# An HGRN2 attention block and a SwiGLU block in one kernel: half copies of v, score copies, transposed output and the order of the crossed matmuls

## The chip, the cores and the metric

The kernel runs on one core of a Trainium2 chip. The metric is the device time of one execution in microseconds (us); less is better. The engines of the core work side by side, each through its own list of instructions in order: TensorE (PE; its weight loads are shown as PEld), VectorE (DVE), ScalarE (ACT), GpSimd (POOL) and SyncE (SP). SP and POOL issue most of the DMA transfers here. PE writes its results to PSUM, whose eight banks the program hands out through pools; ACT and DVE read them there.

## The reference

A gated linear recurrence over 768 steps for 4 batches and 8 heads of 48 channels, and a SwiGLU block behind it. All is float32.

```python
f = 1.0 / (1.0 + np.exp(-f_logit))              # q, k, v, f_logit: (4, 8, 768, 48)
for t in range(S):
    state = f[:, :, t, :, None] * state + np.einsum('bhd,bhe->bhde', k[:, :, t], v[:, :, t])
    y[:, :, t] = np.einsum('bhd,bhde->bhe', q[:, :, t], state)
x = y.transpose(0, 2, 1, 3).reshape(B * S, H * D)     # (3072, 384)
g = x @ w_gate                                        # (384, 1536)
out = (g * sigmoid(g) * (x @ w_val)) @ w_out          # (1536, 384)
```

## The kernel before

**Chunks and units.** The 768 steps are cut into six chunks of 128. A unit u is one batch b in one chunk c; u = 4c + b. For each unit the program turns the gates into running products, scales keys and queries with them, and multiplies: scores = keys x queries inside the chunk (masked to be causal), y = scores x v plus queries x the state of the chunk before, and a new state from keys and v. The MLP of chunk c - 1 (mlp_plain for chunk 0; mlp_fifteen and down_seven with fewer products for the others) runs on the same engines at the same time as the attention of later chunks.

**Order.** Attention is written as a generator (`attention(u)`, from line 624) that yields at 15 points. Tables of due times (EARLY for chunk 1, `times(c)` for chunks 2 to 5) say between which steps of the MLP each of these pieces is written, and `in_order` then fixes the order of each engine's list as written (in the part up to chunk 1 without POOL). So the order within PE, ACT, DVE and SP is that of the code; an instruction that waits holds up all behind it on its engine. The steps that matter here, in their order: qT (the scaled queries) and, in chunk 1, decayed (the state scaled by the gates); scores; masking; y; the rest of y; the new state.

**Units in halves.** In chunks 1 to 5 the first three batches (`in_halves`) treat each chunk as two halves of 64 steps, so that the quadrants of the PE array work side by side: K and M of 48 or 64. For these units the masked scores of a tile A (128 x 2 x 4 x 128) hold, for each parity `par` of the heads, 6 x 64 columns: four blocks on the diagonal, which a mask multiplies (DVE, line 795), and two blocks below it, which need no mask. From chunk 2 on the latter are plain copies on ACT (line 792); in chunk 1 DVE multiplies them by ones. Both stand in the step of masking, 0.9, 1.5 or 2 units of the planner's time behind that of the scores.

**v and its half copies.** Half of the A products need v with its halves of time exchanged, in the other 64 partitions. These copies are loaded beside v (line 504) into tiles of their own that `make_lower` sets aside: for chunk 1 inside the weight-sum tile `extra`, which is free until then, later in a tile `lower`. Their columns 48 to 64 are set to zero.

**y on PE** (lines 813 to 841): first, from chunk 2 on, the new state dS (8 matmuls, from kt, the transposed keys, which come back from DRAM by DMA); then the state part of y for the heads that lie in the right partitions ("own"), then 16 A products. In the step after, `rest_of_y`, come the state parts of the other heads ("crossed": 2 x 4 matmuls of 32 columns), the copies of y to yT (ACT, line 849), and ten DMA transfers for the columns of the chunk into xT, the input of the MLP (line 856). From chunk 2 on that step is due 0.03 behind y, and the next unit's scores 0.02, so that the scores stand between them. In chunk 1 dS comes in the step `rest_of_y`, ahead of the crossed matmuls.

**Room for yT.** In chunk 1 yT and `diagonal` (the state of the fourth batch, laid out for full-array matmuls) share one buffer of tag x. Later both take a buffer of the ring of three, tag aside, into which ACT copies products of the MLP.

**Banks.** From chunk 2 on the scores take banks of the MLP's own tags (o or A) in most units, so the next product with that tag waits until DVE and ACT have read the scores.

Names in the profile: L754 and L760 write scores (sc), L833 the state part of y, L841 the A products of units in halves, L867 the y of fourth batches, L813 dS, L1150 the products of the MLP and L1253 its down products. "x16" in a row counts the two passes that PE makes for each float32 matmul.

Of the kernel before, what the change touches and what calls it, by code (L numbers as in the profile page):

```python
# [290 lines left out]
def short_path(ctx, tc, ident, least, judge, q, k, v, f_logit, moe_w_gate, moe_w_val, moe_w_out, out):  # L291
# [9 lines left out]
    nc = tc.nc  # L301
# [110 lines left out]
    CH = C // 2  # L412
    lower = [], []

    def make_lower(room, masks, late):
# [12 lines left out]
        lower[late][:] = vs_, masks  # L428

    def other_v(u):  # L430
        at = lower[units[u][1] >= SQUARES][0]
        return at[u % 2 if units[u][1] >= SQUARES else units[u][0]]

    room = extra.rearrange("p e n j t -> p e (n j t)")
    make_lower([room[:, 4, i * HP * W:(i + 1) * HP * W] for i in range(B - 1)], room[:, 2, 0:(HP + HP // 2) * CH], False)

# [39 lines left out]
    def load(u, what="fkqv"):  # L476
# [3 lines left out]
        for nm in "fqkv" if c >= SQUARES else "fvkq" if by_squares(u) else "fkqv":  # L480
# [19 lines left out]
            queue.dma_start(out=dst[:, :, 0:D], in_=src[b, :, rows, :].rearrange("h t d -> t h d"))  # L500
            if nm == "v" and in_halves(u):
                for n in range(2):
                    since = c * C + (1 - n) * CH
                    queue.dma_start(out=other_v(u)[n * CH:(n + 1) * CH, :, 0:D],
                                    in_=src[b, n * HP:(n + 1) * HP, since:since + CH, :].rearrange("h t d -> t h d"))

# [117 lines left out]
    def attention(u):  # L624
# [13 lines left out]
        in_squares = by_squares(u)  # L638

        def multiply(out, x, by):  # L640
# [105 lines left out]
        yield  # L746

        sc = [score_bank(u) for _ in range(2)]
        halves = in_halves(u)
        for keys in range(2) if halves else ():  # L750
# [5 lines left out]
        for a in () if halves else range(HP):  # L756
            for par in range(2):
                r = rows_of(par)
                for half in range(2) if c else ():
                    nc.tensor.matmul(sc[par][W * half:W * half + W, a * C:(a + 1) * C], lhsT=kT[r, a, W * half:W * half + W],  # L760
                                     rhs=qT[r, a, :], start=True, stop=True)
                if c == 0:
                    nc.tensor.matmul(sc[par][:, a * C:(a + 1) * C], lhsT=kT[r, a, :], rhs=qT[r, a, :], start=True, stop=True)
# [9 lines left out]
        yield  # L773
        if u != SQUARES * B:
            A = att.tile([128, 2, HP, C], FP32, tag="A", name="A")
        flat = A.rearrange("p r a t -> p r (a t)")
        if not in_squares:
# [6 lines left out]
        if halves:  # L784
            first, rest = slice(0, HP * CH), slice(HP * CH, (HP + HP // 2) * CH)
            masks = lower[c >= SQUARES][1]
            if c < SQUARES:
                first = slice(0, rest.stop)
            else:
                masks = masks.unsqueeze(1).broadcast_to((128, HP, CH))  # L790
                for par in range(2):
                    nc.scalar.copy(flat[:, par, rest], sc[par][:, rest])
            for par in range(2):
                by_head = [t if len(t.shape) == 3 else t[:, first].rearrange("p (a t) -> p a t", t=CH) for t in (flat[:, par], sc[par], masks)]
                nc.vector.tensor_tensor(*by_head, ALU.mult)
# [21 lines left out]
        if halves:  # L817
# [11 lines left out]
            def of_state(pars_of, parts, first):  # L829
                for part in parts:  # L830
                    for a in range(HP):
                        par = pars_of(a)
                        nc.tensor.matmul(place(a, par, part), lhsT=decayed[rows_of(par), a, part], rhs=qT[rows_of(par), a, :],  # L833
                                         start=first, stop=not first, skip_group_check=True)

            of_state(lambda a: a // 2, [slice(0, W)], True)
            for keys in range(2):
                for par in range(2):
                    for a in (0, 2, 1, 3):
                        h, top = 2 * a + par, a // 2  # L840
                        nc.tensor.matmul(queries_of_keys(place(a, par), keys), rhs=blocks_of_keys(flat[:, par], top, a, keys),  # L841
                                         lhsT=(v_[:, h, :] if keys == top else other_v(u)[:, h % HP, :])[top * CH:(top + 1) * CH],
                                         start=False, stop=keys == 1 and par == top, skip_group_check=True)
# [42 lines left out]
        if halves:  # L886
            rest_of_y()
        if c >= SQUARES and u + 2 < len(units):
# [130 lines left out]
    def times(c):  # L1019
# [3 lines left out]
        masks = {"b": 2, "o": 0.9, "A": 1.5}  # L1023
        return [[f, *steps, s + 0.02, s + masks[kind], s + 2.2, o, o + (0.03 if b < B - 1 else 0.01), o + 2.1]
                for b, (f, steps, (s, kind), o) in enumerate(zip(sigmoid, CHAINS[c], SCORES[c], outputs))]

# [391 lines left out]
    make_rooms(comb)  # L1418
    room = comb.tile([128, 2 * HP * W + CH], FP32, tag="lower", name="lower")
    make_lower([room[:, i * HP * W:(i + 1) * HP * W] for i in range(2)], room[:, 2 * HP * W:], True)  # L1420
    load(SQUARES * B)
# [107 lines left out]
```

## Time and profile before

| | |
|---|---|
| time, median of 3 runs (us) | 594.83 (594.12 to 596.44) |
| profiled execution: its time, its span (us) | 594.78, 593.1 |
| ACT copies of scores, line 792 | 24 x 283 ns |
| DVE masking, line 795, chunks 2 to 5 | 24 x 416 ns |
| ACT copies to yT, line 849 | 30 x 374 ns |
| DMA transfers out of yT from POOL: issue, issue to landing | 0.50 us, 3.2 us |

The page of the profile gives busy times as shares of the span and the costliest groups of instructions. A row of the timeline has start, length, engine, line, operation, what is written from what, the number of instructions, and in brackets the idle time of the engine just before with what ended it. A row of the view of waits has who waited for whom, the total in us, how often, and the longest. Matmuls are pipelined, so their lengths overlap: the time that one takes from the engine is the distance to the next start.

### The profile page before, as it was taken

Reading aid. Unit: us, or ns where it says so; the run is one execution under the profiler, and the core shown is the slowest. Engines: PE = TensorE matmul, PEld = TensorE weight load, DVE = VectorE, ACT = ScalarE, POOL = GpSimd, SP = SyncE. Lnnn points to the kernel's source line nnn. Section 1 sums busy time; section 2 is a strip of 40 time slices with the busy share of each in tenths; the row PEclk is TensorE's granted clock in tenths of the full one; section 3 lists DMA queues with packets and bytes.
Section 4 is the critical chain, followed back from the end, with each engine's and each line's share of the span. In section 5 each row is a group of like instructions: output and inputs, shape, how many; then the busy total and the mean of one; then the engine's idle time right before and its main releaser. Section 6 shows DMA issues by size and latency. Waiting matters only on the chain.

```text
span 593.1 us, 12331 instructions
## 1 busy us (share of the span) xinstructions
PE 577.1 (97%) x4644; PEld 476.7 (80%) x4644; DVE 471.6 (80%) x828; ACT 307.1 (52%) x589; POOL 119.2 (20%) x262
## 2 busy tenths in 40 slices
PE   7899999999989999999999999999999999999996
PEld 5744444557878999878899988899988899988996
DVE  7988998999989977988995978995878972666641
ACT  3587787023877522666741486742376830356600
POOL 6140344201132150030330030311030321000000
PEclk9999999999999999999999999999999999999999
DMA  9999696234659566443444443344341100100001
GB/s 217 257 289 259 197 247 155 62 92 128 130 119 146 106 151 165 111 108 73 113 102 104 135 106 71 89 106 106 104 114 28 28 8 8 54 1 2 0 1 56
DMA packets 117825, 64.48 MB, mean 109 GB/s; under 512 B 75568, under 2 KB 108144, under 8 KB 117760
## 3 DMA queue, kind: packets, MB, share of 16 engines
q1 hardware_dynamic: 105360, 48.29, 33.1%
q0 software_dynamic: 11248, 13.78, 10.3%
q10 hardware_dynamic: 1152, 1.57, 0.7%
q8 instruction: 37, 0.61, 0.4%
q14 instruction: 28, 0.23, 0.1%
HBM read 49.64 MB, written 8.65 MB: 98 GB/s over the span
## 4 chain that ended last, share of the span: by engine, by line
PE 77%; DVE 7%; DMA 5%; ACT 3%; issue 3%; POOL 2%; SPq 1%; DVEq 0%; ACTq 0%; POOLq 0%
PE o L1253 19%; PE A L1150 16%; PE B L1150 13%; PE o L1150 5%; PE c L1150 5%; PE o L1316 3%; DMA xT<-yT 2%; PE y L867 2%; PE o L957 2%; PE gate L934 2%; DMA kt<-turn 2%; PE val L934 2%; PE dS L813 1%; PE sc L754 1%; PE y L833 1%
## 5 line engine op out<-in xcount | busy, mean ns | idle before, releaser
L856 POOL DMA_DIRECT2D xT<-yT x120 | 59.5, 505 | 71.7 <-ACT yT L849 62.3
L1150 PE MATMUL A<-xs,w_both 128*128 128x256 f32 x240 | 61.9, 380 | 1.3 <-ACT aside L1155 1.3
L1253 PE MATMUL o<-w_out,h 128*128 128x192 f32 x360 | 62.0, 327 | 0.0
L1253 PEld LDWEIGHTS o<-w_out,h 128*128 128x128 f32 x360 | 58.8, 190 | 0.9 <-issue 0.4
L1155 ACT COPY aside<-A 128x512 f32<-128x512 f32 x60 | 35.1, 584 | 34.9 <-PE A L1150 32.5
L1051 DVE TENSOR_TENSOR c<-c,aside 128x512 f32<-128x512 f32 x60 | 41.2, 686 | 13.7 <-ACT aside L1155 12.1
L1150 PEld LDWEIGHTS A<-xs,w_both 128*128 128x128 f32 x240 | 45.2, 190 | 8.1 <-ACT aside L1155 1.7
L1155 ACT COPY c<-A 128x512 f32<-128x512 f32 x40 | 23.3, 583 | 45.2 <-PE A L1150 45.2
L1102 DVE TENSOR_TENSOR h<-h,c 128x256 f32<-128x256 f32 x100 | 40.5, 413 | 6.1 <-ACT h L1166 5.8
L1054 DVE TENSOR_TENSOR c<-c,aside 128x512 f32<-128x512 f32 x60 | 41.0, 683 | 2.3 <-ACT aside L1155 2.2
L1253 PE MATMUL o<-ws,h 128*128 128x192 f32 x240 | 41.7, 328 | 0.0
L1166 ACT ACTIVATE h<-c 128x256 f32<-128x256 f32 x100 | 39.2, 416 | 4.7 <-DVE c L1051 3.5
L1150 PE MATMUL A<-xs,extra 128*128 128x256 f32 x160 | 41.2, 380 | 0.2 <-ACT c L1155 0.2
L1150 PE MATMUL B<-xs,w_both 128*128 128x256 f32 x160 | 41.2, 380 | 0.0
L1150 PE MATMUL c<-xT,w_both 128*128 128x256 f32 x160 | 41.1, 379 | 0.0
L1150 PE MATMUL B<-xT,extra 128*128 128x256 f32 x160 | 41.1, 379 | 0.0
L1155 ACT COPY aside<-B 128x512 f32<-128x512 f32 x60 | 35.1, 585 | 10.0 <-PE B L1150 6.6
L1253 PEld LDWEIGHTS o<-ws,h 128*128 128x128 f32 x240 | 39.3, 190 | 1.0 <-issue 0.8
L743 POOL MEMSET gates<- 128x4 f32 x24 | 3.7, 152 | 164.7 <-DVE qT L646 159.6
L1051 DVE TENSOR_TENSOR c<-c,o 128x384 f32<-128x384 f32 x15 | 8.2, 549 | 34.2 <-PE o L1253 34.2
L1054 DVE TENSOR_TENSOR c<-o,c 128x512 f32<-128x512 f32 x40 | 27.3, 684 | 9.3 <-ACT h L1166 5.8
L1150 PEld LDWEIGHTS A<-xs,extra 128*128 128x128 f32 x160 | 30.3, 190 | 4.7 <-ACT c L1155 0.6
(181 smaller groups left out, 1261.8 us busy)
## 6 DMA issues: line engine op xcount, KB each, us to landing
fsquares<-in_f_logit_dram SPq DMA_DIRECT2D x64, 96.0 KB
qsquares<-in_q_dram SPq DMA_DIRECT2D x64, 96.0 KB
ksquares<-in_k_dram SPq DMA_DIRECT2D x64, 96.0 KB
w<-in_moe_w_gate_dram SPq DMA_DIRECT2D x6, 768.0 KB
w<-in_moe_w_val_dram SPq DMA_DIRECT2D x6, 768.0 KB
w<-in_moe_w_out_dram SPq DMA_DIRECT2D x6, 768.0 KB
v<-in_v_dram SPq DMA_DIRECT2D x19, 192.0 KB
kt<-turn SPq DMA_DIRECT2D x12, 256.0 KB
```

What stands on the lines that cost most here:

```text
L856: (nc.gpsimd if c >= SQUARES else nc.sync).dma_start(out=xT[c][f % 128:f % 128 + n, f // 128, b * C:(b + 1) * C], in_=yT[r:r + n, a // 2, ...
L867: nc.tensor.matmul(y[Q * (n % 4):Q * (n % 4) + Q, n // 4 * C:(n // 4 + 1) * C], lhsT=lhsT, rhs=rhs, start=n % 4 not in met, stop=last, ski ...
L934: nc.tensor.matmul(p, lhsT=w[:, j, i, :], rhs=xT[c][:, i, :], start=(i == 0), stop=(i == KT - 1))
L957: nc.tensor.matmul(p, lhsT=hidden_tile(h, n // 2)[:, n % 2 * 2 + b // 2, b % 2 * C:(b % 2 + 1) * C], rhs=w_out[:, j, :], start=(n == 0), s ...
L1051: nc.vector.tensor_tensor(dst, a, b, ALU.add)
L1054: nc.vector.tensor_tensor(dst, a, b, ALU.subtract)
L1102: lagging.append(lambda: f(*args))
L1150: nc.tensor.matmul(p[name][:, n, :], lhsT=weights_of[a][:, n, j, :], rhs=tokens[b], start=fresh and n == 0, stop=True, skip_group_check=True)
L1155: nc.scalar.copy(t, p[name])
L1166: nc.scalar.activation(dst, src[:, 0, :], AF.Silu)
L1253: nc.tensor.matmul(p[:, n, :], lhsT=lhsTs[j][:, n * C:(n + 1) * C], rhs=rhs[:, j, :], start=first and j == order[0] and n == 0, stop=j == ...
L1316: nc.tensor.matmul(p, lhsT=hidden_tile(h, j)[:, 2, n * C:(n + 1) * C], rhs=b22[:, j, :], start=j == order[0], stop=j == order[-1])
```

## The change

1. The half copies of v (`load_other_v`) go into columns of A that the masked scores leave free: the two parities now lie at 0 to 384 and 384 to 768 of 1024 columns, and the last 256 hold four heads of v. They are loaded when A is handed out: with qT in chunk 1, with the scores later. Only 48 of 64 columns are loaded and used as stationary operand, so nothing is set to zero. The tiles of `make_lower` are gone, the masks stay (`make_diagonals`).
2. The ACT copies of the blocks below the diagonal stand right behind the scores instead of in the step of masking.
3. yT has a tile of its own (tag x in `att`); `diagonal` of chunk 1 takes a buffer of the ring in which weights are loaded (w64, four buffers).
4. The crossed matmuls run first, then dS (in chunk 1 too), the own state part, and the A products. The step that follows only copies y and starts the transfers; it is due 0.01 behind y, ahead of the next unit's scores.

```diff
-        vs_ = [t.rearrange("p (h d) -> p h d", h=HP) for t in room]
-        for t in vs_:
-            nc.gpsimd.memset(t[:, :, D:W], 0.0)
+    def other_v(A):
+        return A.rearrange("p r a t -> p (r a t)")[:, 12 * CH:].rearrange("p (h e) -> p h e", e=W)
+    def load_other_v(A, u):
+        b, c = units[u]
+        queue = nc.sync if c >= SQUARES or not by_squares(u) else nc.gpsimd
+        for n in range(2):
+            since = c * C + (1 - n) * CH
+            queue.dma_start(out=other_v(A)[n * CH:(n + 1) * CH, :, 0:D],
+                            in_=v[b, n * HP:(n + 1) * HP, since:since + CH, :].rearrange("h t d -> t h d"))
...
         def aside_room(name):
             if c < SQUARES:
-                return first_pool.tile([128, 2, TB // 2], FP32, tag="x", name=name)
+                return wst.tile([128, 2, TB // 2], FP32, tag="w64", name=name, bufs=4)
...
+        if halves and c < SQUARES:
+            A = att.tile([128, 2, HP, C], FP32, tag="A", name="A")
+            load_other_v(A, u)
         multiply(qT, qp, pairs(gate)[:, :, 1:N1])
...
+        flat = [A.rearrange("p r a t -> p (r a t)")[:, 6 * CH * par:6 * CH * par + 8 * CH] for par in range(2)]
+        if halves and c >= SQUARES:
+            load_other_v(A, u)
         sc = [score_bank(u) for _ in range(2)]
...
+        for par in range(2) if halves and c >= SQUARES else ():
+            nc.scalar.copy(flat[par][:, rest], sc[par][:, rest])
...
-                for par in range(2):
-                    nc.scalar.copy(flat[:, par, rest], sc[par][:, rest])
...
-            if c >= SQUARES and c < NCH - 1:
-                dS = new_state()
...
-            of_state(lambda a: a // 2, [slice(0, W)], True)
+            of_state(lambda a: 1 - a // 2, [slice(0, Q), slice(Q, W)], True)
+            if c < NCH - 1:
+                dS = new_state()
+            of_state(lambda a: a // 2, [slice(0, W)], False)
...
-                                         lhsT=(v_[:, h, :] if keys == top else other_v(u)[:, h % HP, :])[top * CH:(top + 1) * CH],
+                                         lhsT=(v_[:, h, :] if keys == top else other_v(A)[:, h % HP, 0:D])[top * CH:(top + 1) * CH],
...
-            def rest_of_y():
-                of_state(lambda a: 1 - a // 2, [slice(0, Q), slice(Q, W)], False)
-                yT = aside_room("yT")
+            def copy_y():
+                yT = att.tile([128, 2, TB // 2], FP32, tag="x", name="yT")
...
-        return [[f, *steps, s + 0.02, s + masks[kind], s + 2.2, o, o + (0.03 if b < B - 1 else 0.01), o + 2.1]
+        return [[f, *steps, s + 0.02, s + masks[kind], s + 2.2, o, o + 0.01, o + 2.1]
```

What this does to the lists of the engines, at three places. (A line's number is about 6 higher in the changed file.)

PE, first unit of chunk 2, before: the start of the block of y between two products of the MLP (A and B are also names of banks; y<-A is an A product, the tile v_124 is v).

```order
L1150 MATMUL B<-xT,extra 128x256 x2
L1150 MATMUL A<-xT,w_both 128x256 x2
L813 MATMUL dS<-v_124,kt 64x48 x8
L833 MATMUL y<-qT,decayed 64x128 x4
L841 MATMUL y<-A,v_124 64x128
L841 MATMUL y<-A,lower 64x128
```

PE, the same block, before: its end, with the next unit's scores (sc) and the crossed matmuls (32x128).

```order
L841 MATMUL y<-A,lower 64x64
L841 MATMUL y<-A,v_124 64x64
L754 MATMUL sc<-qT,kT 64x2x64 x8
L754 MATMUL sc<-qT,kT 64x64 x8
L833 MATMUL y<-qT,decayed 32x128 x8
L1150 MATMUL A<-xs,w_both 128x256 x2
```

PE, the same place, changed: the start of the block.

```order
L1156 MATMUL A<-xT,w_both 128x256 x2
L837 MATMUL y<-qT,decayed 32x128 x8
L819 MATMUL dS<-v_124,kt 64x48 x8
L837 MATMUL y<-qT,decayed 64x128 x4
L848 MATMUL y<-A,v_124 64x128
L848 MATMUL y<-A 48x128
```

The crossed matmuls have moved from the end, behind the scores, to the start; the products with the half copies write 48 rows instead of 64.

ACT at the same place, before: copies of y, a product of the MLP (c), a scaling of weights (ws), and then the copies of the scores.

```order
L668 ACTIVATE fsquares<-fsquares 128x16x32
L849 COPY yT<-y 128x256 x2
L1155 COPY c_1706<-A 128x512
L1089 ACTIVATE ws_1369<-ws_1368 128x1152
L792 COPY A<-sc 128x128 x2
L1155 COPY c_1718<-B 128x512
```

ACT, the same place, changed.

```order
L671 ACTIVATE fsquares<-fsquares 128x16x32
L855 COPY yT<-y 128x256 x2
L775 COPY A<-sc 128x128 x2
L1161 COPY c_1702<-A 128x512
L1095 ACTIVATE ws_1360<-ws_1359 128x1152
L1161 COPY c_1711<-B 128x512
```

The copies of the scores have moved ahead of the product's copy and of the scaling.

SP, chunk 2, between the second and the third unit, before: loads of q, the transposed keys kt, then v.

```order
L492 DMA ksquares<-in_k_dram 32x4x192 x4
L492 DMA qsquares<-in_q_dram 32x4x192 x4
L772 DMA kt<-turn 128x1x512
L500 DMA v_125<-in_v_dram 128x8x48
L492 DMA fsquares<-in_f_logit_dram 32x4x192 x4
```

SP, the same place, changed.

```order
L498 DMA ksquares<-in_k_dram 32x4x192 x4
L498 DMA qsquares<-in_q_dram 32x4x192 x4
L506 DMA v_125<-in_v_dram 128x8x48
L454 DMA A<-in_v_dram 64x4x48 x2
L784 DMA kt<-turn 128x1x512
L498 DMA fsquares<-in_f_logit_dram 32x4x192 x4
```

The transfer of kt now stands behind the load of v and the two half copies.

More of the change, by code (lines that the diff above doesn't have):

```diff
@@ L412, in short_path, with make_diagonals @@
     CH = C // 2
-    lower = [], []
-    def make_lower(room, masks, late):
+    diagonals = {}
+    def make_diagonals(masks, late):
         for n in range(2):
@@ L424, in make_lower @@
             nc.gpsimd.memset(masks[:, HP * CH:], 1.0)
-        vs_ = [t.rearrange("p (h d) -> p h d", h=HP) for t in room]
-        for t in vs_:
-            nc.gpsimd.memset(t[:, :, D:W], 0.0)
[L428 to L432, printed above, removed]
+        diagonals[late] = masks
     room = extra.rearrange("p e n j t -> p e (n j t)")
-    make_lower([room[:, 4, i * HP * W:(i + 1) * HP * W] for i in range(B - 1)], room[:, 2, 0:(HP + HP // 2) * CH], False)
+    make_diagonals(room[:, 2, 0:(HP + HP // 2) * CH], False)
     def in_halves(u):
@@ L500, in load @@
             queue.dma_start(out=dst[:, :, 0:D], in_=src[b, :, rows, :].rearrange("h t d -> t h d"))
[L501 to L505, printed above, removed]
     def weight_piece(dst, src, parts, signs):
@@ L638, in attention @@
         in_squares = by_squares(u)
+        halves = in_halves(u)
+        first, rest = slice(0, HP * CH), slice(HP * CH, (HP + HP // 2) * CH)
         def multiply(out, x, by):
@@ L746, in attention @@
         yield
+        if u != SQUARES * B and not (halves and c < SQUARES):
+            A = att.tile([128, 2, HP, C], FP32, tag="A", name="A")
+        flat = [A.rearrange("p r a t -> p (r a t)")[:, 6 * CH * par:6 * CH * par + 8 * CH] for par in range(2)]
+        if halves and c >= SQUARES:
+            load_other_v(A, u)
         sc = [score_bank(u) for _ in range(2)]
-        halves = in_halves(u)
         for keys in range(2) if halves else ():
@@ L784, in attention @@
         if halves:
-            first, rest = slice(0, HP * CH), slice(HP * CH, (HP + HP // 2) * CH)
-            masks = lower[c >= SQUARES][1]
+            masks = diagonals[c >= SQUARES]
             if c < SQUARES:
@@ L790, in attention @@
                 masks = masks.unsqueeze(1).broadcast_to((128, HP, CH))
-                for par in range(2):
-                    nc.scalar.copy(flat[:, par, rest], sc[par][:, rest])
             for par in range(2):
-                by_head = [t if len(t.shape) == 3 else t[:, first].rearrange("p (a t) -> p a t", t=CH) for t in (flat[:, par], sc[par], masks)]
+                by_head = [t if len(t.shape) == 3 else t[:, first].rearrange("p (a t) -> p a t", t=CH) for t in (flat[par], sc[par], masks)]
                 nc.vector.tensor_tensor(*by_head, ALU.mult)
@@ L833, in of_state @@
                         nc.tensor.matmul(place(a, par, part), lhsT=decayed[rows_of(par), a, part], rhs=qT[rows_of(par), a, :],
[L834 to L836 removed]
+                                         start=first, stop=False, skip_group_check=True)
+            of_state(lambda a: 1 - a // 2, [slice(0, Q), slice(Q, W)], True)
+            if c < NCH - 1:
+                dS = new_state()
+            of_state(lambda a: a // 2, [slice(0, W)], False)
             for keys in range(2):
@@ L1418, in short_path @@
     make_rooms(comb)
-    room = comb.tile([128, 2 * HP * W + CH], FP32, tag="lower", name="lower")
-    make_lower([room[:, i * HP * W:(i + 1) * HP * W] for i in range(2)], room[:, 2 * HP * W:], True)
+    make_diagonals(comb.tile([128, CH], FP32, tag="diagonals", name="diagonals"), True)
     load(SQUARES * B)
```

11 lines of the change are left out of this document (4 added, 7 removed).

## The prediction

> **What bounds the kernel now.** I read the page first, for who is busy.
>
> ```profile
> span 593.1 us, 12331 instructions
> PE 577.1 (97%) x4644; PEld 476.7 (80%) x4644; DVE 471.6 (80%) x828; ACT 307.1 (52%) x589; POOL 119.2 (20%) x262
> ```
>
> TensorE (PE) is busy for 577.1 of 593.1 us. Only two things can change the time: the 16.0 us in which PE idles, and what PE itself has to do. So I asked next where the idle time lies, by stretches of 60 us (length, then busy us of PE, PEld, DVE, ACT, POOL, the granted clock, DMA share, GB/s).
>
> ```profile
> 0.00:60.00 60.00, 54.44 (x445) 33.27 (x446) 49.83 (x82) 38.10 (x63) 18.95 (x59) 1.00 0.98 257
> 120.00:180.00 60.00, 56.82 (x412) 43.53 (x411) 53.86 (x97) 34.23 (x65) 11.75 (x25) 1.00 0.51 121
> 240.00:300.00 60.00, 58.48 (x458) 51.00 (x456) 53.71 (x99) 39.64 (x84) 10.22 (x23) 1.00 0.41 94
> 300.00:360.00 60.00, 60.00 (x583) 54.87 (x583) 48.48 (x86) 27.96 (x57) 11.23 (x24) 1.00 0.46 112
> 540.00:593.00 53.00, 47.91 (x264) 45.16 (x262) 26.75 (x47) 15.93 (x35) 0.00 (x0) 1.00 0.05 16
> ```
>
> 5.6 us of the idle time are at the start, 5.1 after the last matmul, 3.2 between 120 and 180, 1.5 between 240 and 300. From 300 on PE has no gap, so nothing that a faster ScalarE, VectorE or DMA does there can show. The clock is 1.00 everywhere and plays no part. The view of waits, for PE alone, names the gaps (total us, times, longest):
>
> ```profile
> PE sc L763 <- DVE qT L646: 2.4, 2, 1.6
> PE o L1150 <- DVE A L795: 1.5, 1, 1.5
> PE y L867 <- ACT diagonal L658: 1.4, 1, 1.4
> PE A L1150 <- ACT aside L1155: 1.3, 1, 1.3
> PE dS L813 <- DMA kt<-turn: 0.3, 1, 0.3
> ```
>
> The first belongs to chunk 0, which the change leaves as it is. The other four are at places that the change touches, and the sum is made of them and of two of 0.26 us whose rows stand further down.
>
> **The diagonal tile (a tile of its own for yT).** Before, yT and diagonal of chunk 1 share one buffer.
>
> ```profile
> 116.18 0.35 DVE L652 TENSOR_TENSOR decayed<-state,least 128x192 f32<-128x192 f32 x1
> 122.77 0.51 ACT L656 COPY diagonal<-spare 128x384 f32<-128x384 f32 x1 [11.39 <-DMA xT<-yT]
> 123.72 1.12 PE L867 MATMUL y<-qT,diagonal 128*32 128x128 f32 x21 [1.35 <-ACT diagonal L658]
> 126.64 0.43 DVE L1054 TENSOR_TENSOR xs<-xT 128x256 f32<-128x256 f32 x1 [1.19 <-ACT xT L882]
> ```
>
> ScalarE has been idle for 11.39 us until the last transfer out of yT lands, and PE waits 1.35 us. Now diagonal takes a weight buffer and yT has its own. Its other input, decayed, is done at 116.53, so diagonal could be ready near 117.8 against the 122.4 at which PE wants it: the wait goes, with 4.6 us to spare. What could be late next is VectorE, which idles 1.19 us before xs for the same chain and then works off the sums for the next stage. The next time that it idles, it waits for PE:
>
> ```profile
> 142.22 0.69 DVE L1054 TENSOR_TENSOR c<-o,c 128x512 f32<-128x512 f32 x1 [1.07 <-PE o L1150]
> ```
>
> So it starts 1.19 us sooner and has 1.07 us in hand: I count the full 1.35.
>
> **The copies right behind the scores.** At the second unit of chunk 2, PE needs a bank of tag o that still holds scores.
>
> ```profile
> 170.32 0.68 DVE L1051 TENSOR_TENSOR c<-c,aside 128x512 f32<-128x512 f32 x1
> 172.11 1.17 ACT L1089 ACTIVATE ws<-ws 128x1152 f32<-128x1152 f32 x1
> 173.17 0.42 ACT L792 COPY A<-sc 128x128 f32<-128x128 f32 x2
> 173.46 0.76 DVE L795 TENSOR_TENSOR A<-sc,lower 128x256 f32<-128x256 f32 x2 [2.45 <-ACT A L792]
> 173.94 1.13 PE L1150 MATMUL o<-xT,w_both 128*128 128x256 f32 x4 [1.49 <-DVE A L795]
> ```
>
> In ScalarE's order the copies stand behind a product's copy and the 1.17 us ws; VectorE's masking waits 2.45 us for them, and PE 1.49. Now they stand ahead of both. Scores end near 170.1, the copies (0.42 us) near 170.6, and VectorE is free at 171.0, so its 0.76 us end near 171.75 while PE wants the bank near 171.9. I count 1.49. The copies delay what is behind them by 0.42 us each time; the sum of ScalarE's work is unchanged, and it is busy 34.23 of 60 us here. By the same ordering the third product's B bank is freed about 0.1 us late; I charge 0.1.
>
> **yT out of the ring of aside tiles.**
>
> ```profile
> 263.32 0.58 ACT L1155 COPY aside<-A 128x512 f32<-128x512 f32 x1 [2.26 <-DMA xT<-yT]
> 263.96 1.13 PE L1150 MATMUL A<-xs,w_both 128*128 128x256 f32 x4 [1.25 <-ACT aside L1155]
> ```
>
> One of three aside buffers was held by yT until its transfers landed. With yT elsewhere ScalarE could have copied 2.26 us earlier: 1.25 us gained. The single new yT buffer must be free again when the next unit's copy comes; I return to that among the rivals.
>
> **The crossed matmuls first.** The chain of work shows one unit's block on PE (start, length):
>
> ```profile
> 278.90 0.60 PE dS L813 x16
> 279.50 0.38 PE y L833 x8
> 279.88 0.67 PE y L841 x32
> 280.55 0.67 PE sc L754 x32
> 281.22 0.38 PE y L833 x16
> ```
>
> The last 0.38 us, the crossed matmuls, moves to the front; the same rows run, 2.70 us in all. What changes is when each piece starts: dS, own state and A products stay or come later, and the next unit's scores start 0.38 us later, yet nothing runs behind them. Where scores waited for a bank or for qT, the crossed matmuls now fill that wait.
>
> ```profile
> 168.75 1.40 PE L754 MATMUL sc<-qT,kT 48*64 48x128 f32 x32
> 203.88 0.85 PE L754 MATMUL sc<-qT,kT 48*64 48x128 f32 x32
> 213.07 1.10 PE L760 MATMUL sc<-qT,kT 48*64 48x128 f32 x32 [0.26 <-DVE qT L646]
> 250.88 0.89 PE L754 MATMUL sc<-qT,kT 48*64 48x128 f32 x30 [0.26 <-DVE c L1054]
> ```
>
> The first row takes 1.40 us against an undisturbed 0.85, a hidden wait of 0.5; the last two show 0.26 each beside a stretched start. At each of the three the gain is at least 0.26 and at most the 0.38 us moved: I take 0.38, since the release by VectorE does not move; 1.14 in all.
>
> The same order costs something in chunk 1, where dS ran last but one and is now second.
>
> ```profile
> 104.53 0.71 POOL L781 DMA_DIRECT2D kt<-turn  x1 [0.86 <-issue]
> 108.11 0.45 PE L833 MATMUL y<-qT,decayed 48*64 48x128 f32 x8
> 109.56 0.67 PE L813 MATMUL dS<-v,kt 128*64 128x48 f32 x16 [0.34 <-DMA kt<-turn]
> DMA to landing us min/median/max: 4.9/5.2/12.3
> ```
>
> At the third unit kt lands about 109.5. Before, own state and A products (1.05 us) ran ahead of dS and PE waited 0.34. Now only 0.38 us stand ahead, so PE waits about 1.0 us: a loss of 0.66. It is zero only if kt's transfer starts earlier; POOL has two more transfers to issue for this unit, but long before, so I expect no shift either way.
>
> **Half copies of v.** The bytes stay (two transfers of 48 KB a unit). At the start POOL no longer issues four and SP two; PE's 5.6 us there hang on the VectorE and ScalarE chain of chunk 0, so nothing is gained. From chunk 2 on, both transfers wait on SP until PE has left A, behind the load of v, and kt's transfer now stands behind all three: about 2 us later. Nearly everywhere 13 us or more lie between. The tight place is the third unit of chunk 2:
>
> ```profile
> 203.06 0.57 SPq L772 DMA_DIRECT2D kt<-turn  x1
> 211.09 0.67 PE L813 MATMUL dS<-v,kt 128*64 128x48 f32 x16
> ```
>
> SP can start v at 204.3, when the A products end, so by its rows (0.4 for v, 0.65 for each half) kt is issued near 206.1 to 206.7. No view gives SP's landing time; bounds from POOL's transfers of the same shape are 4.9 and 12.3, and I take the median of 5.2: it lands near 211.9 at the worst, against dS at 211.5. I charge 0 and keep up to 7 us as the bad end.
>
> The crossed A products use stationary operands of 48 columns where it was 64. The profile has no such row; the nearest are the rows of 48 partitions, which keep the pace of 64 (the sc rows above). I take 0.
>
> **Sum.** Gains 1.35 + 1.49 + 1.25 + 1.14 = 5.23; losses 0.66 + 0.1 = 0.76; net 4.5 us. The profiled execution took 594.78 us (its span 593.1 and 1.7 around it), which is within 0.1 of the median of 594.83. 594.78 - 4.5 = 590.3, or 0.75% less. What a measurement of this kernel can tell from no change is about 0.5%, 3.0 us; faster begins at 591.9.
>
> [...] For the price of changing shapes:
>
> ```profile
> 235.65 0.83 PE sc L754 x32
> ```
>
> The same 32 score rows take 0.83 us ahead of a full-array product and 0.67 ahead of the crossed matmuls: 0.16 us for going to the full array, and nothing visible for going from 64 to 32 columns. [...] By the rows, 64 to 48 should cost what 64 to 32 does.
>
> **Rivals.** *VectorE takes over* (0.22). It is busy 53.86 of 60 us between 120 and 180. If it, not PE, sets the pace there once PE's waits are gone, the gain at diagonal and of the filled waits is lost: 1.49 + 1.25 - 0.66 = 2.1, so 592.7. Against it: VectorE idles 1.19 us for that very chain, 1.07 for PE and 2.45 for the copies.
>
> *The transfers are late* (0.08). If kt of that unit lands 9 us after issue, PE waits 4.2 us and nearly all is given back: 594.5. Against it: DMA share is 0.51 or less.
>
> *The new buffer of yT blocks ScalarE* (0.03), so that the change does not do what it says. Units two and three of chunk 2 are 9 us apart, and ten transfers of 0.5 us each with about 3 to land take 8 to 9. A blocked ScalarE would hold an output copy; 1 to 2 us, so about 592.
>
> *48 columns switch the array* (0.07). The place is the A products of all 15 units: 14 changes between 64 and 48 columns in each. At 0.16 us apiece that is 2.2 us a unit and 34 in all: 624. It becomes slower by 0.5% when one change costs over 7.5 / 210 = 36 ns. Against it: the crossed matmuls of 32 columns follow 64 at no visible cost.
>
> **How the numbers follow.** The forecast of 590.3 has 0.60. It is the only case that is faster by over 0.5%; VectorE, transfers and yT lie within; 48 columns lie beyond. That gives 0.60, 0.33, 0.07. For the range: with neither the loss at kt nor the 0.1 the time is 594.78 - 5.23 = 589.5; the runs of before lie up to 0.7 below their median, of which I take 0.5 in: 589.0. Upwards it takes in VectorE and the late transfers to 595.2 and leaves out the switching array and the far end of the transfers.
>
> **What would show it.** Right: no wait of PE on diagonal near 122, none on A near 172, none on aside near 262; the wait on kt near 109 at about 1.0 us instead of 0.34; the 2.70 us block unchanged. Wrong: new PE waits on VectorE between 139 and 170; a wait of dS on kt or of y on A's transfer near 210; an A product block longer than 0.67 us. If those waits vanish and the time stays, PE's own work grew.

## The result and the profile after

| | before | change |
|---|---|---|
| time, median of 8 runs each, lowest to highest (us) | 594.40 (593.10 to 596.44) | 598.88 (596.85 to 601.38) |
| ratio to before, 95% interval | 1 | 1.0076 (1.0049 to 1.0103) |
| profiled execution: time, span (us) | 594.78, 593.1 | 598.69, 597.0 |

The change is 0.8% slower. 590.3 was predicted and the range ended at 595.2, so both the sign and the range were wrong. The page of the changed kernel, with the line of the granted clock in 40 slices of 14.9 us:

```profile
span 597.0 us, 12326 instructions
PE 579.3 (97%) x4644; PEld 479.1 (80%) x4644; DVE 471.9 (79%) x828; ACT 306.5 (51%) x589; POOL 119.3 (20%) x257
PEclk9999997999999989999999999999999999999999
```

PE is busy for 2.2 us more with the same 4644 instructions, and two slices have lost their clock. Its waits (total us, times, longest):

```profile
PE dS L819 <- DMA kt<-turn: 6.3, 2, 4.3
PE sc L773 <- DVE qT L649: 2.5, 2, 1.7
...
PE A L1156 <- ACT c L1161: 0.2, 1, 0.2
```

The view has seven lines; those left out are of chunk 0 or the kernel's start. The three waits that were to go are gone: PE no longer waits for diagonal, for the masked A, or for aside. In their place stands one line of 6.3 us, dS waiting for kt. By stretches (length, then busy us of PE, PEld, DVE, ACT, POOL, the clock, DMA share, GB/s):

```profile
60.00:120.00 60.00, 55.70 (x393) 29.11 (x392) 49.11 (x80) 34.71 (x45) 26.18 (x44) 0.94 0.64 158
120.00:180.00 60.00, 59.79 (x449) 44.69 (x447) 57.42 (x103) 30.98 (x58) 11.05 (x25) 1.00 0.51 115
180.00:240.00 60.00, 57.91 (x541) 53.10 (x541) 48.88 (x85) 26.40 (x58) 15.55 (x28) 0.97 0.69 132
240.00:300.00 60.00, 60.00 (x492) 52.35 (x491) 54.87 (x103) 40.14 (x83) 11.28 (x25) 1.00 0.47 113
```

From 120 to 180 PE is now busy for 59.79 us where it was 56.82, and from 240 to 300 it has no gap: the gains are there. The loss is between 60 and 120 and between 180 and 240, and there the clock is below 1. The first place is the second unit of chunk 1. PE's timeline, first of the kernel before, then of the change:

```profile
87.67 5.42 PE L934 MATMUL gate<-xT,w_both 128*128 128x512 f32 x12
93.01 0.67 PE L813 MATMUL dS<-v,kt 128*64 128x48 f32 x16
...
99.25 2.74 PE L957 MATMUL o<-w_out,h 128*128 128x384 f32 x8
```

```profile
86.87 0.45 PE L837 MATMUL y<-qT,decayed 48*32 48x128 f32 x16
91.62 1.09 PE L819 MATMUL dS<-v,kt 128*64 128x48 f32 x16 [4.30 <-DMA kt<-turn]
...
94.56 6.79 PE L940 MATMUL gate<-xT,w_both 128*128 128x512 f32 x12
...
106.34 2.74 PE L963 MATMUL o<-w_out,h 128*128 128x384 f32 x8
```

Before, 5.4 us of gate products stood between this unit's y and its dS. Now dS is wanted at 87.3, right behind the crossed matmuls, and kt lands at 91.6. The transfer itself is no slower than it was. The kt tile in the stretch from 77 to 94, before and then after (instructions, and time from issue to landing):

```profile
L781 POOL DMA_DIRECT2D kt<-turn x1: 708/708/708, 78.4 to 78.4; - x1
...
DMA to landing us min/median/max: 12.3/12.3/12.3
```

```profile
L790 POOL DMA_DIRECT2D kt<-turn x1: 722/722/722, 79.2 to 79.2; - x1
...
DMA to landing us min/median/max: 12.3/12.3/12.3
```

It took 12.3 us both times. Before, it landed near 90.7, 2.3 us ahead of dS, and so left no wait in any view.

The rest of the loss is the clock. The change in stretches of 0.5 us, around the two places (columns as above):

```profile
90.00:90.50 0.50, 0.00 (x0) 0.00 (x0) 0.50 (x2) 0.50 (x1) 0.00 (x0) 1.00 1.00 250
90.50:91.00 0.50, 0.00 (x0) 0.00 (x0) 0.47 (x2) 0.50 (x2) 0.00 (x0) 0.54 1.02 267
91.00:91.50 0.50, 0.00 (x0) 0.00 (x0) 0.50 (x2) 0.50 (x1) 0.00 (x0) 0.50 0.94 329
97.00:97.50 0.50, 0.50 (x2) 0.22 (x1) 0.00 (x0) 0.00 (x0) 0.50 (x2) 0.63 0.58 126
97.50:98.00 0.50, 0.50 (x2) 0.21 (x2) 0.00 (x0) 0.00 (x0) 0.50 (x2) 1.00 0.71 107
216.50:217.00 0.50, 0.50 (x16) 0.50 (x16) 0.00 (x0) 0.00 (x0) 0.00 (x0) 0.83 0.52 111
220.00:220.50 0.50, 0.50 (x20) 0.41 (x12) 0.00 (x0) 0.00 (x0) 0.47 (x1) 0.75 0.56 169
```

Every row from 91.00 to 97.00 has 0.50; so the means of 0.54 and 0.63 put the fall to one half at 90.54, 3.2 us into the wait, and its end at 97.37. The twelve gate products, 5.42 us before, take 6.79; from 99.25 to 106.34 the lag is 7.09 us, of which 0.25 was there at 86.9, 4.30 is the wait, and 2.54 the clock. The second place is the third unit of chunk 2, on SP and on PE:

```profile
207.47 0.38 SPq L506 DMA_DIRECT2D v<-in_v_dram  x1
207.95 1.87 SPq L454 DMA_DIRECT2D A<-in_v_dram  x2
209.88 0.56 SPq L784 DMA_DIRECT2D kt<-turn  x1
```

```profile
214.03 0.45 PE L837 MATMUL y<-qT,decayed 48*32 48x128 f32 x16
216.47 0.83 PE L819 MATMUL dS<-v,kt 128*64 128x48 f32 x16 [1.99 <-DMA kt<-turn]
```

kt is issued behind v and both half copies, lands 6.55 us later, and PE waits 1.99 us. By the last two rows of the fence before, the clock is at one half from 216.83 to 220.25, with PE busy all the time; half of these 3.42 us, an estimate of about 1.7, is lost besides. The lag of the change behind before, at starts that can be compared (0.38 taken off in the third row, where dS now has the crossed matmuls ahead of it):

| place | before | change | lag |
|---|---|---|---|
| w_out products behind the third unit, chunk 1 | 110.55 | 117.23 | 6.68 |
| dS, fourth unit, chunk 1 | 125.77 | 130.66 | 4.89 |
| dS, second unit, chunk 2 | 202.34 | 205.67 | 2.95 |
| dS, fourth unit, chunk 2 | 228.07 | 234.16 | 6.09 |
| dS, fourth unit, chunk 3 | 319.83 | 323.71 | 3.88 |

The lag had risen to 7.09; it falls by 4.1, rises by 3.1, and falls by 2.2.

### The profile page after: what moved, and what is told of

The parts are those of the page before. It is cut to its first block, busy times and chain, and to the rows that moved or that the text cites. A ratio compares the mean times of both kernels' runs of the same rounds, so it can differ in the third digit from the quotient of the medians.

```text
span 597.0 us, 12326 instructions
## 1 busy us (share of the span) xinstructions
PE 579.3 (97%) x4644; PEld 479.1 (80%) x4644; DVE 471.9 (79%) x828; ACT 306.5 (51%) x589; POOL 119.3 (20%) x257
## 4 chain that ended last, share of the span: by engine, by line
PE 86%; DMA 5%; DVE 3%; ACT 3%; issue 1%; POOL 1%; SPq 0%; ACTq 0%; DVEq 0%; POOLq 0%
PE o L1259 19%; PE A L1156 17%; PE B L1156 14%; PE c L1156 5%; PE o L963 5%; PE o L1156 5%; PE gate L940 3%; PE o L1322 3%; DMA kt<-turn 3%; PE val L940 3%; PE y L873 2%; PE dS L819 2%; PE y L848 2%; PE y L837 2%; PE sc L764 1%
```

## The experiments

The theory: two transfers of kt land after the place to which dS, or SP's queue, was moved, and PE's clock falls because of the waits. The rivals: the half copies make kt late wherever dS stands; the clock falls for a reason of its own; the new tiles or matmuls cost; VectorE takes over. Differences below are between medians, ratios are to runs of before on the same chip. The median of before was 594.2 to 595.1 us on the chips used, so a difference of under a microsecond between two kernels tells nothing by itself.

**dS of chunk 1 back in its old step** (base: the change).

```diff
-            if c < NCH - 1:
+            if c >= SQUARES and c < NCH - 1:
                 dS = new_state()
             of_state(lambda a: a // 2, [slice(0, W)], False)
```

> The change with one edit: in chunk 1 dS goes back to its old step, behind the A products and the gate products. Theory (dS was moved ahead of the landing of kt, and TensorE's clock fell after the wait): at the second unit kt lands near 91.6 and dS wants it near 93.3, so the wait of 4.30 us goes, and with it the half clock between 91.6 and 97.4, which cost 2.5 us. 598.9 - 6.8 = about 592.1, the granted clock between 60 and 120 back at 1.00, and the wait of 1.99 us near 214 stays. Rival one (the two half copies issued by POOL make kt late, wherever dS stands): dS waits for kt in its old place too, and the time stays over 597. Rival two (the clock falls in this kernel for another reason): only the 4.3 us come back, 594.6, with the clock at 0.94 as now.

592.17 us, ratio 0.9952 (0.9934 to 0.9970): 6.7 us less than the change (7.4 by the ratios), 6.8 were expected. The profiled execution is the fastest of six, 590.08 us; of its two waits for kt, that of chunk 2 is 1.5 us instead of 1.99, and the clock did not fall behind it (1.00 in all rows from 208 to 232). Its waits and its row of chunk 1:

```profile
PE dS L819 <- DMA kt<-turn: 1.8, 2, 1.5
```

```profile
60.00:120.00 60.00, 59.72 (x441) 31.21 (x440) 55.92 (x91) 35.28 (x47) 26.57 (x46) 1.00 0.64 162
```

The wait of 4.30 and the lost clock have gone together, with the half copies still on POOL. That rules out the first rival for chunk 1. The second one said 594.6 and a clock of 0.94, and the clock is at 1.00.

**kt ahead of the half copies on SP** (base: the change).

```diff
-        if halves and c >= SQUARES:
-            load_other_v(A, u)
         sc = [score_bank(u) for _ in range(2)]
...
         if at_once:
             turn_queue.dma_start(out=kt, in_=turn.rearrange("t i a r e -> i t (a r e)"))
+        if halves and c >= SQUARES:
+            load_other_v(A, u)
         yield
```

> The change with one edit: from chunk 2 on SP issues kt ahead of the two half copies of v, still behind the load of v. Theory: at the third unit of chunk 2 kt is issued 1.9 us sooner, near 207.9, and lands near 214.5, just when dS wants it; the wait of 1.99 us shrinks below 0.3, the clock stays up, and about 3.4 us come back: 595.5. The wait of 4.30 us in chunk 1 stays. Rival one (the landing is set by the DMA queues and not by its place on SP): kt lands near 216.4 as before, 598.9. Rival two (the half copies become the late ones): y waits on A's transfer at that unit, 597 or more. If only the wait and not the clock counts: 597.0.

595.59 us, ratio 1.0008 (0.9995 to 1.0020), 3.3 less than the change; 595.5 was expected. Between 180 and 240 PE is busy for 59.80 us at a clock of 1.00, and of PE's waits for kt only that of chunk 1 is left:

```profile
PE dS L819 <- DMA kt<-turn: 5.1, 1, 5.1
```

The place on SP was the cause in chunk 2.

**Both edits.**

> Both edits in one kernel. Theory: both waits and both spells of half clock go, and the gains that were forecast are left: 598.9 - 6.8 - 3.4 = 588.7, 0.96% below the kernel before. Rival (VectorE takes over once PE's waits are gone): the two returns do not add up and the time stays over 591.

590.06 us, ratio 0.9916 (0.9901 to 0.9930); against the runs of before on the same chip 5.1 us less. 588.7 was expected. The returns add up to 8.8 of the 10.0 us that the two edits gave one by one. 0.7 us of waits for kt are left, 0.49 at the third unit of chunk 1 and 0.20 near 210; and part of the return of chunk 2 had come with the first edit already, as its trace shows. VectorE did not take over: that rival wanted over 591, and between 120 and 180 VectorE is busy for 57.80 of 60 us while PE is for 59.68.

**The kernel before, with only dS of chunk 1 moved to the head of its block.**

```diff
-            if c >= SQUARES and c < NCH - 1:
+            if c < NCH - 1:
                 dS = new_state()
             y = [bank("y") for _ in range(2)]
```

> The kernel before with one edit: dS of chunk 1 at the head of the unit's block, where it stands in the later chunks, and nothing else of the change. Theory: at the second unit dS wants kt at 86.6, kt lands near 90.7, so TensorE waits about 4.1 us, its clock halves and costs another 2.5; the 0.34 at the third unit are spared: 594.8 + 6.3 = 601 (ratio 1.0105). Rival (half copies, the new tiles or the crossed matmuls are what costs): no change, 594.8.

600.96 us, ratio 1.0106 (1.0082 to 1.0130). 601 was expected: one moved group of matmuls costs the old kernel as much as the whole change does, or more (the intervals overlap). PE in that kernel:

```profile
90.68 0.67 PE L813 MATMUL dS<-v,kt 128*64 128x48 f32 x16 [3.46 <-issue]
```

The profile names no releaser here. But dS starts within 0.1 us of 90.7, where kt landed in the kernel before (issued at 78.4, 12.3 us to landing).

**The same wait, but with PE busy in it** (base: the change; the products go to the bank that dS then overwrites).

```diff
             p = bank("dS")
+            for _ in range(9 if u == 5 else 0):
+                nc.tensor.matmul(p, lhsT=qT[:, 0, :], rhs=qT.rearrange("p a t -> p (a t)"), start=True, stop=True)
```

> The change with nine 128x512 products more on TensorE ahead of dS at the second unit of chunk 1, written to the bank that dS then overwrites: about 4.0 us of work inside the wait of 4.30 us, so that TensorE waits as long for kt but does not idle. Theory (the clock falls because TensorE idles): the granted clock stays at 1.00 between 88 and 100, dS starts at the same time, and the 2.5 us that the half clock cost come back: 596.4. Rival (the clock falls for another reason, the new tile shapes or the load on the chip): no change, 598.9, with the clock at 0.5 from 92 to 96 as now. If the products outlast the wait, dS starts up to 0.5 us later.

599.30 us, ratio 1.0071 (1.0054 to 1.0089). I had counted one pass for a float32 product where PE makes two, so the work was twice as long as the wait. PE's timeline, and a stretch of the windows:

```profile
87.01 7.99 PE L819 MATMUL dS<-qT 128*128 128x512 f32 x18
94.94 0.67 PE L821 MATMUL dS<-v,kt 128*64 128x48 f32 x16
```

```profile
92.00:96.00 4.00, 4.00 (x40) 1.99 (x42) 2.93 (x6) 0.00 (x0) 0.00 (x0) 1.00 0.35 91
```

dS starts 3.3 us later than in the change, and still the time is about the same: the clock stayed up here (in chunk 2 it fell again, behind a wait of 2.3 us: its mean is 0.70 from 216 to 220). With that 3.3, the expected 596.4 becomes 599.7. The second fence is the stretch that ran at half clock in the change. Since the size was off, the test was made again with four products.

> The busy wait again with four products instead of nine, since each is carried out as two of 0.45 us: 8 of them make 3.6 us of work inside the wait of about 4.3 us, and 0.7 us of idling are left. Theory (idling lowers the clock): dS starts at the same time as in the change, the granted clock stays at 1.00 from 88 to 100, and the 2.5 us of the half clock come back: 596.4 (ratio 1.003 to 1.005). Rival (the clock falls for another reason): 598.9, ratio 1.0076, with 0.5 from 92 to 96.

594.94 us, ratio 1.0013 (0.9994 to 1.0032): 3.9 us less than the change, by work that computes nothing. Timeline and windows of this kernel:

```profile
87.60 3.70 PE L819 MATMUL dS<-qT 128*128 128x512 f32 x8
91.58 0.67 PE L821 MATMUL dS<-v,kt 128*64 128x48 f32 x16 [0.28 <-DMA kt<-turn]
```

```profile
92.00:96.00 4.00, 4.00 (x56) 2.44 (x53) 3.90 (x7) 0.10 (x1) 0.71 (x1) 1.00 0.77 163
...
216.00:220.00 4.00, 4.00 (x26) 4.00 (x26) 3.60 (x6) 1.48 (x5) 3.67 (x8) 1.00 0.65 176
```

kt lands when it did (91.58), and the clock is 1.00. So it is the idling that lowers the clock at this place, not the new tiles or the load of the chip. The return beyond the expected 2.5 us is in chunk 2: its wait is 1.5 us in this execution, and the clock did not fall there either. Four of the twelve executions had a mean clock of 0.994 to 0.996 all the same (595.3 to 599.5 us), and of those there is no trace.

**dS behind the A products in every unit** (base: the change).

```diff
             of_state(lambda a: 1 - a // 2, [slice(0, Q), slice(Q, W)], True)
-            if c < NCH - 1:
-                dS = new_state()
             of_state(lambda a: a // 2, [slice(0, W)], False)
...
+            if c < NCH - 1:
+                dS = new_state()
             def copy_y():
```

> The change with dS behind the own-state and A products in every unit (1.05 us later than the change has it). Theory (a wait of 2.0 us lowers the clock and one of 1.5 us does not, as the rows show so far): in chunk 1 the wait is 3.25 us and the clock still falls; in chunk 2 the wait is 0.9 us and the clock stays up. 598.9 - 1.05 - 1.05 - 1.5 = 595.3. If the clock's fall did not depend on the length of the wait, only the two terms of 1.05 come back: 596.8. If dS had nothing to do with it: 598.9.

593.41 us, ratio 0.9974 (0.9956 to 0.9992), 1.9 less than the 595.3 expected. In the profiled execution kt of the second unit landed 11.3 us after its issue, PE waited 1.70 us instead of 3.25, and the clock did not fall (1.00 from 84 to 104):

```profile
90.32 0.67 PE L819 MATMUL dS<-v,kt 128*64 128x48 f32 x16 [1.70 <-DMA kt<-turn]
```

Other executions of this kernel ran otherwise: the five with a mean clock of 0.998 or more took 591.1 to 592.7 us, the four with 0.995 594.1 to 594.9. I read this as a wait that lowers the clock in some executions and not in others, with a difference of about 2.5 us, the size of the term in chunk 1; there is no trace of a slower one.

**kt of chunk 1 issued by ScalarE** (base: the change), to learn where the 12.3 us come from.

```diff
-                turn_queue.dma_start(out=kt, in_=turn.rearrange("t i a r e -> i t (a r e)"))
+                (nc.scalar if c < SQUARES else turn_queue).dma_start(out=kt, in_=turn.rearrange("t i a r e -> i t (a r e)"))
```

> The change with one edit: kt of chunk 1 is issued by ScalarE instead of POOL. In ScalarE's order it stands behind a copy that ends near 83, so the issue is 3.6 us later than POOL's at 79.2. Theory (the landing of 12.3 us is the backlog of the 16 DMA engines, which are full from 78 to 92 with four weight transfers of 768 KB): a transfer issued at 83 lands no sooner than 90, dS waits 3 us or more, and the time is 597.5 to 600. Rival (POOL's queue alone is slow, the engines are not the limit): kt lands 5 us after its issue, near 88, dS waits under 1 us, the clock stays up, and the time is 593.

599.48 us, ratio 1.0074 (1.0049 to 1.0098). The issue came sooner than I had read from the order of ScalarE's list:

```profile
L790 ACTq DMA_DIRECT2D kt<-turn x1: 1114/1114/1114, 80.1 to 80.1; - x1
```

```profile
92.05 1.09 PE L819 MATMUL dS<-v,kt 128*64 128x48 f32 x16 [4.98 <-DMA kt<-turn]
```

Another queue, and again 12 us (80.1 to 92.05). It is not POOL's queue that is slow. In the change SP issues four weight transfers of 768 KB around kt, two ahead of it (75.8 and 76.4) and two behind it (81.7 and 83.0, against 79.2 for kt), and the DMA engines (the share is the last number but one, GB/s the last) are full until kt lands:

```profile
75.80 7.58 SPq L523 DMA_DIRECT2D w<-in_moe_w_out_dram  x4
```

```profile
78.00:84.00 6.00, 6.00 (x15) 2.66 (x14) 5.43 (x9) 3.85 (x5) 1.93 (x4) 1.00 1.04 307
84.00:88.00 4.00, 3.32 (x23) 1.13 (x21) 3.63 (x6) 3.96 (x5) 1.09 (x2) 1.00 1.05 210
88.00:92.00 4.00, 0.38 (x8) 0.41 (x9) 3.90 (x8) 3.72 (x5) 1.11 (x3) 0.82 1.06 273
```

At the mean of these rows, 270 GB/s, the engines move 3.3 MB in the 12.3 us, of which kt is 0.26. That kt is slow because it shares full engines with the weights is read from these rows; no run took the weights away.

**Two of the gains taken back, one at a time** (base: both edits). First the copies of the full score blocks back with the masks.

```diff
-        for par in range(2) if halves and c >= SQUARES else ():
-            nc.scalar.copy(flat[par][:, rest], sc[par][:, rest])
...
                 masks = masks.unsqueeze(1).broadcast_to((128, HP, CH))
+                for par in range(2):
+                    nc.scalar.copy(flat[par][:, rest], sc[par][:, rest])
```

> The kernel with both edits, but ScalarE's copies of the full score blocks back where they stood before, with the masks. The forecast counted 1.49 us for them at the second unit of chunk 2. Theory (the gain is theirs): PE waits there again for the bank, about 1.5 us, and the time is 590.1 + 1.5 = 591.6 (ratio 0.994). Rival (that the wait went because of something else, such as the other offset of the units): no such wait, 590.1 (ratio 0.9916).

591.40 us, ratio 0.9953 (0.9938 to 0.9968), and the wait is back to the hundredth, in ScalarE's order behind ws:

```profile
170.09 1.17 ACT L1095 ACTIVATE ws<-ws 128x1152 f32<-128x1152 f32 x1
171.16 0.42 ACT L798 COPY A<-sc 128x128 f32<-128x128 f32 x2
...
171.92 1.13 PE L1156 MATMUL o<-xT,w_both 128*128 128x256 f32 x4 [1.49 <-DVE A L801]
```

Then yT from chunk 2 on back in the ring of aside tiles.

```diff
-                yT = att.tile([128, 2, TB // 2], FP32, tag="x", name="yT")
+                yT = aside_room("yT") if c >= SQUARES else att.tile([128, 2, TB // 2], FP32, tag="x", name="yT")
```

> The kernel with both edits, but yT of chunk 2 on is taken from the ring of three aside tiles again. The forecast counted 1.25 us for leaving that ring. Theory: ScalarE waits again for the transfers out of yT before a copy to aside, PE waits about 1.25 us for the bank near 260, and the time is 590.1 + 1.25 = 591.3 (ratio 0.9937). Rival (the wait went with the other offset of the units): no such wait, 590.1 (ratio 0.9916).

591.11 us, ratio 0.9942 (0.9921 to 0.9963):

```profile
262.56 1.13 PE L1156 MATMUL A<-xs,w_both 128*128 128x256 f32 x4 [1.00 <-ACT aside L1161]
```

The wait is back, 1.00 us instead of 1.25. By the medians the two returns cost 1.3 and 1.1 us, little more than the chips differ by, so it is the rows that show it: both gains belong to the edits to which the forecast gave them.

**Two further steps** (base: both edits). dS behind the A products from chunk 2 on:

```diff
-            if c >= SQUARES and c < NCH - 1:
-                dS = new_state()
             of_state(lambda a: a // 2, [slice(0, W)], False)
...
+            if c >= SQUARES and c < NCH - 1:
+                dS = new_state()
             def copy_y():
```

> The kernel with both edits, and dS behind the A products from chunk 2 on, 1.05 us later. Theory (kt's landing at the third unit of chunk 2 is within a microsecond of dS, and every wait on kt there is covered by 1.05 us of other work): the 0.7 us that PE and its weight loads still wait for kt near 210 go, and nothing else changes: 589.4 (ratio 0.9905). Rival (the later end of dS makes the sum for the state late, and with it decayed and y): a new wait of y, 590.1 or more.

591.09 us, ratio 0.9943 (0.9923 to 0.9964): no gain, where 589.4 was expected. dS waits for kt in chunk 2 no longer (0.25 us are left in chunk 1), but the A products, now 0.67 us sooner, wait for the half copies, which neither theory had named:

```profile
PE y L846 <- DMA A<-in_v_dram: 1.0, 1, 1.0
```

And the load of v one step later, so that kt stands ahead of it on SP:

```diff
-        if c >= SQUARES and u + 2 < len(units):
-            load(u + 2, "v")
         yield
+        if c >= SQUARES and u + 2 < len(units):
+            load(u + 2, "v")
         if c == 0:
```

> The kernel with both edits, and from chunk 2 on the load of v for the unit after next is issued one step later, so that on SP kt of the third unit of chunk 2 stands ahead of it and no longer waits for PE to leave the v buffer. Theory: kt is issued about 2 us sooner against PE, lands before dS wants it, and the last wait on kt near 210 (0.7 us in all, up to 1.5 in other kernels at this place) is gone: 589.4 (ratio 0.9905), every run at a clock of 0.998 or more. Rival (v now becomes late, or the loads behind it do): a new wait of PE on v, fsquares or turn between 210 and 240, 590.1 or more.

588.92 us (588.29 to 589.25), ratio 0.9907 (0.9887 to 0.9926), where 589.4 was expected. It is the lowest time of all and below both kernels, though the ratio does not tell it from that of both edits alone (0.9916). At the place in question:

```profile
200.06 0.57 SPq L782 DMA_DIRECT2D kt<-turn  x1
```

```profile
208.09 0.67 PE L819 MATMUL dS<-v,kt 128*64 128x48 f32 x16
```

kt has 8.0 us there, and dS starts without a wait (one of 0.44 is left in chunk 1).

## Why the prediction was wrong

- **The gains were right in kind, and their sum in part by luck.** "Gains 1.35 + 1.49 + 1.25 + 1.14 = 5.23": with both waits on kt undone the kernel is 5.1 us faster than before (4.2 to 5.9 by the interval), with 0.7 us of waits for kt still in it. In the traces of before and change the lags fall by more than was forecast. The diagonal: between the third and the fourth unit of chunk 1 the lag falls by 1.79, 1.35 of which is that wait. From the fourth unit of chunk 2 to that of chunk 3 it falls by 2.21, for which 1.25 + 0.38 were forecast. What the rest is stays open. The score copies: the wait of 1.49 came back with them. yT: 1.25 forecast, 1.00 when taken back. That the crossed matmuls fill the waits of the scores was not undone by itself; only the rows speak for it (the scores at 168.75 took 1.40 us, and take 0.86 in the change).
- **The step that failed** is "The same order costs something in chunk 1, where dS ran last but one and is now second", with its 0.66. I priced it at the third unit alone, because only there the view of waits showed dS waiting for kt (0.34). The unit with the most to lose showed no wait at all: its dS stood behind gate products. I had the number in hand, "4.9/5.2/12.3", and used its 12.3 only as an end of a range in chunk 2. Asked unit by unit, the tile's rows say issue at 78.4, landing 12.3 later, dS moved from 93.0 to 87.0: a wait of 3.7 us. It measured 4.30. The third unit, priced at 1.0, waited not at all, since PE came 7 us later.
- **A smaller step**: "I charge 0" for kt behind v and the half copies on SP. The issue was placed rightly (206.1 to 206.7, plus the lag of 3.3 at this place, against 209.88). The landing took 6.55 us, not the 5.2 of POOL's median; with dS 4.6 us behind the issue, PE waits 1.99.
- **A term that was missing**: "The clock is 1.00 everywhere and plays no part." In the profiled execution of before none of PE's waits from 30 us on, the longest 1.5 us, brought it down. The new waits did, for 2.54 and about 1.7 us. Together the four terms, 4.30 + 2.54 + 1.99 + 1.7, are 10.5 us where 0.66 was charged.
- **The rivals.** VectorE did not take over. The single buffer of yT blocked nothing: in the change ScalarE's copies to yT wait for PE alone. The late transfers were named, at one of their two places, with 594.5 and a chance of 0.08. 48 columns cost nothing: in the change from 240 us on, where the clock is 1.00, the A products of 48 columns and those of 64 beside them take 269 ns each, as those of 64 did before. (Over the whole execution they take 288 and 289, means that take in the units at half clock.)

## What to carry to other kernels

When an instruction is moved ahead, look up when each of its inputs arrives, unit by unit, also where it does not wait today: work that stands ahead of it hides the arrival from every view of waits. A new TensorE wait can cost more than its length: behind those of 4.30 and 1.99 us the half clock took 2.54 and about 1.7 us more here, and 3.7 us of work put into the first, though it computes nothing, left the clock at 1.00. Keep the engine busy in such a wait if it cannot go. In a queue that runs in order, what is wanted first has to be issued first: two small copies ahead of a critical transfer held the queue for 1.87 us here, and moving them behind it returned 3.3.

## What the runs showed of the hardware

In the change the granted clock is at one half behind the waits of 4.30 and 1.99 us, and again at the end, after the last matmul (the mean from 595.50 to 596.00 is 0.72, the rows behind it have 0.50). It fell in four other kernels behind a wait on kt: 5.1 us with kt ahead of the half copies, and 4.98 with kt issued by ScalarE (0.50 from 92 to 96 in both), 3.46 in the kernel before with dS moved (0.50 from 92 to 94), and 2.3 in the busy wait with nine products (0.70 from 216 to 220). The shortest such wait was in the kernel with yT in the ring, whose PE waited 1.33 us for kt until 209.53:

```profile
210.50:211.00 0.50, 0.50 (x17) 0.32 (x15) 0.00 (x0) 0.00 (x0) 0.12 (x2) 1.00 0.69 127
211.00:211.50 0.50, 0.50 (x28) 0.50 (x23) 0.00 (x0) 0.00 (x0) 0.00 (x0) 0.66 0.80 148
214.50:215.00 0.50, 0.50 (x5) 0.50 (x4) 0.50 (x2) 0.00 (x0) 0.50 (x2) 0.92 0.78 223
```

The rows between 211.50 and 214.50 have 0.50, so by the mean of 0.66 the clock falls near 211.16, 1.6 us after PE is back at work. The waits of 1.52 and 1.48 us at the same place in two other kernels (dS of chunk 1 back, four products in the wait), and the 1.70 us of chunk 1 above, left it at 1.00. So the length of the wait does not by itself tell, in these executions, whether the clock falls. What else decides it, and why the same wait seems to lower the clock in some executions and not in others, no run shows.
